# A two-layer attention and token-MLP kernel: the masks of one probability tile untied, and a new order written out by hand

## The chip, the cores and the metric

The kernel runs on one core of a Trainium2 chip. The core has five engines, each with an instruction queue of its own that it works through strictly in order: TensorE (PE, matrix products), VectorE (DVE), ScalarE (ACT), GpSimd (POOL) and SyncE (SP), which here only issues DMAs. Engines wait for one another by semaphores. The metric is the device time of one execution in microseconds; the median over several runs is compared.

## The reference, cut to what matters

```python
def _A_ref(x, wqkv, wo):                # S = 2048, D = 512
    H = 32; Dh = D // H; W = 256
    q, k, v = ...                       # x @ wqkv, 32 heads of 16
    scores = jnp.einsum("bhqd,bhkd->bhqk", q, k) * (Dh ** -0.5)
    mask = (idx[:, None] - idx[None, :] >= 0) & (idx[:, None] - idx[None, :] < W)
    p = _softmax(jnp.where(mask, scores, -1e9))
    return (p @ v, heads joined) @ wo

def _B_ref(x, w1, b1, w2, b2):          # F = 1792, mixes tokens, not features
    h = _layernorm(x)
    u = _gelu(jnp.einsum("bsd,sf->bdf", h, w1) + b1)
    return transpose(jnp.einsum("bdf,fs->bds", u, w2) + b2)

for layer in range(2):                  # the same weights in both
    x = x + _A_ref(_layernorm(x), wqkv, wo)
    x = x + _B_ref(_layernorm(x), w1, b1, w2, b2)
```

All arrays are bfloat16. Attention is causal with a window of 256 tokens, so of the 2048 x 2048 scores only a band is computed.

## The kernel before

The 2048 tokens are 16 tiles of 128; x stays in SBUF in place. Each layer's work comes in these kinds:

- **Normalise.** `ln_blocks`: statistics (L478) and their aggregate (L480) on VectorE, `rstd` (L491) on GpSimd, then `normalise` (L498) on VectorE, which writes `xh_sb`.
- **Project.** `qkv(m)` handles token block m of 512 tokens. Transposes of `xh_sb` are DMAs on SyncE (L549), or for the first block of a layer products with an identity on TensorE (L556). Then q, k and v by dense products (L520 and L522; v at L626). A key tile must be spread into a block-diagonal form with zeros between (`kbd`): for the first block straight from PSUM (L586, L588); for later blocks a copy to `stg` (L597, L599), and from there `f_kz`, eight small DMAs on SyncE (L606), or `f_kz2`, two instructions on GpSimd or VectorE (L611).
- **Attend.** `attention` works on chunks of 4 or 8 sub-blocks of 64 queries. A group of scores (L689) fills two pairs of PSUM banks; two exponentials (L704, ScalarE) write one probability tile `pt`; one or two masks (L722, GpSimd) multiply the parts of the tile at the edge of the band by 0 or 1; the products of probabilities and values (L738) follow. The value tiles carry columns of ones, so that the same product gives the sum for the softmax. `od` (L758, VectorE) transposes the result, a reciprocal (L762) and a product (L764, GpSimd or VectorE) scale it, and a last transpose (L769) makes `oT`. There are 304 exponentials, 268 masks and 64 such products in the program.
- **Mix.** `wo_block` adds the attention's output (L780). The token MLP is split: parts of its first product (`u_part`, L520) run as filler under the attention, the rest (`u_last`, L859) after it, then Gelu (L874); its second product (`y_block`, L886) of layer 0 runs under the attention of layer 1, that of layer 1 ends the program. Weights w1 and w2 are loaded by SyncE (L794, L806) into buffers that are used again and again.

The order of all this isn't that of the source. `Graph.op` records each operation with its reads and writes, from which it takes its dependences, and with a `cost`; `replay` then goes through the operations in the order that the packed string `ORDER` holds, which also picks the engine where an operation has alternatives (`alts`). So both the queue of every engine and the buffer that each tile gets are fixed by that string. The string was found off line; the costs and issue times (`cost`, `issue`) in the source are what that search used, and do nothing on the chip.

Waits follow from the recorded keys. `emit` puts a wait before an operation for each engine whose result it needs, its own engine included (TensorE with itself excepted). A mask reads and writes the two keys of its probability tile, so a second mask of that tile is recorded as depending on the first:

```python
op("gpsimd:mask", f_mask, reads=keys + LD, writes=keys, cost=100 + 2.03 * 2 * reps * nc_ * 64)
```

although the two touch different columns. Where a tile has a first mask and a second, the second waits on GpSimd's own semaphore. `f_pv`, the product of probabilities and values, waits for the last writer of the tile.

Of the kernel before, what the change touches and what calls it, by code (L numbers as in the profile page):

```python
# [11 lines left out]
P = 128  # L12
# [1 line left out]

ORDER = (
    'c-',
    'qZYKZxVX9Uj@U@8*RGOh5q@^FRj^P@zH(^gsaxR45MxRH#tlLIf9n;KBhFDqJ|Q0TCQ<;X;K2E>x&+;lhOr6)s%3*usSi7cLywfD03@*y4&UuE',
    '<Yo@2>aua_^EyNPc*w(fs}W`Mz&f8B&B$|2pvfKe!$W6E{Yk$hGkI-y_%c0@w5q#=<ZR(=fjEe2;p)q>HqBw{hQWiRQca$40XOzx~d4Tn8^a*H',
    '-7qv)NMDRm`ytHkl05L#nDm%?h01LEJH#{Yg<2X{#`dBFh>{77L-Z+Dgmp^@5&I4KEBm+hw}x+LmJKif!N9hOsvlOHqiS-',
    '0S!EA5h%yPqM79c5cyar<*Fu2ERM5*Xw3;z32N~5CjXu&^FtR#>JY-vNE5{W{$&^ah?|wE1wG4RBw%es*k4IP4Bw*c7;~UB$0!3xm=d>a_)K5E',  # L20
    'wqmBPpnB{sfF{-',
    'R1H<3lp4u{vGmBUncQr~j1L;UUfO2cR!dPrIZ~R7R&&)^HlnD|W*Rz7qG&K^^`rbIZ#LzuJDW9vI1a<09WbApoYSuxz8ApafRK<7O(Vpp5@;HG',
    '>mQWNHSM@N926o{TU8f)Uz&z#X+zE}!q}g+EHe#4$#oZs)oR_}D~i!rt>|8nDd+N($g(NR`gFSAD+*H>%d!mPbxsH=Ib;N5Ox}Ur-',
    '5p2t<|aF=w%grqo6R%GX+ehL-EO&CZkL<1n{MK?vsteg+wQhsBTZW^7YSr+u}DzzZgrfKzpu+OpH3%}MOjWJvn=x_#dJ3I2Hx1V^Dr#(-',
    '`R4W=Yv6aaDCnHr>rTPjlSFpjb>uRNjHhQQDnp&a+~b;NkY24E@?2!(q-',
    'MT9LF^X5vG1P7{(7`E5zFETEcZrLDaX?>HOQ7tiIJWt`S96(jk*&l3u%R_n=IvixoHO7?DABx6ueZ*Ymun)F~BIsGh64=vH%G%2moOe0N7=UAJ',
    'UxS(sp%$&4-M3$-',
    'juS(Xb~Hb$cqCXAq8bh~XPRISz0HSYUD2mf`!h2RcAUsYv%mGxJB6~Ln>1|~?y8e{Kq0!Q)N+gqX0Erk<coWgW^1&1h#s!k4IYf2aymn*u==xu',
    '-x!y_RW&+~kmAJA$)FN<P~kc24k`PvX7Uiz5M5GTHm5YX3PZpCz@Af$2*(>^R0`S=~}cA+yKjUkMV*2b2QQIa&9VQ5;WADF&r+NNnB#9%9KTCw',
    'MvrfOT`l5<TFnnF3yN`}2HYcL26?E6uYP{UKGEQGLaUm&$IAg>Xa&{!-',  # L30
    'Ms4T?@%OET%7@7m{s+bw&4Z=bN)1PC{yRs@gRwTez{eHj4dJ66T5o4aF{O*pwQ`0JE>GiHZ*uXdcrUxEi90a`xjeWnIgT7202V<>))HsfH6jaF',
    '}wyh|x4#h(NTMeSn98Iw-Rnrt3JQfH!Hs_ouilQG8+GzsmhHfGas)6R3u1%pN!(o3s()Fde=p-',
    'xEH0Oh&7}$<|jR*c@f*6th3f^O(3C7rOnd3Oe{Q*Qu0p>Z*;pRqR2$AV#qx1E8G~yU9`@h6^b~P>+WoJU$lSy+rH_f2P&7X}ct7Jg8ZETKFhK5',
    '534oU3#I%7RH=tBup*Nty(;+Qp^d8-vO)@fth#+9pH90XqAx7&@js;M+=+qPx-x&^TJTuTVbT;wncsUkkUzrQ!Xv-IQfXnVI6@D8$JIhJLZ<_8',
    '}X#rJ;!H-T&X%>{S;squb18rmKVgP1@8fMQ*%o9HfF7-#c>;OHT=T<-',
    'Upw);(?E_QouGa8LH>+Slx%^ImGs4Z*v`8SK@BAhqM((}~!38?RU4yd`Y?G^oXo-',
    '@6q3MFJZrXSE`@*d@Cq^hIcA>RcDISd&ajQXRD#R}mLcexWKmPO1w&$3n;1bz_0ec=1;RuuWsd>*x@h=)3FgrFpZ1l+QO1A#i&AeL<E$WWAfnQ',
    'Msk_7l9xg>d%j&aoZ9Fyq6aOoy8I6XF<v(isjrijs;rZgzgJ2}KbeMh*hJ(eW4_`~7}6B;+q^vRbVG_EYeGHlNLtWR}dPs2Gig0LZM>GK@6Miy',
    'mCD0Q^iQT@N?Hu-)O@gG;v6YH=u;8@fU?u;Zj5cqz-Oh@xoI@qj=L&*KnL;CV+(poZwUpSZr)@a_&<&%^F&z1eKm?#6JOo0Zp{qs4SKt1f7Lxm',
    'p?pNN-{Q+4_|Jsy6`Wra$yjmM{t;(r$ZEM^)P`+NM<I+_qiUb{$Y94#@PTv#I(Plm$eF7w7}V*OFw**f?oYB|X5X4d-',  # L40
    'iAX$cS>A;EQlKJdXBBZN^zaT65<#Mo%MNK}eB9Cn9E;w4=_@ZDyo>3d}*z-CeX@8I^VWCZYn#qf+Z4fw1_YGRs}YDApLc}s3)J)-',
    ')4paQQgnU?qEw%n8f$B2Lq2(hA8QRyvIWkr_DVV>XRyVV2g(Q<!WOvl|(4)qqmBZP+GXwaKZr)Y^{3JP%3DQEz(Su{=|S4?LeCLANyES*^pZvY',
    'oSG#cp|hWxg4OKmh7S{R0)#WJFxrwnO`Ae&dZtW^P21{<OO#H6Rkk57@neq=lRxa2hd;e{XjB?(s}4?l$J=fCIUtM{8XZ_dqn{b|=1%{S-',
    'PoBFHMzj|)fUU-FHe1280J$+w&I^6Tv)z#HQ2h6XXhR%^)Nmo_pDa2D+&SAaWr*=vMdVYQKq|5Kqyvy13f9d1XTY6ettK6xb+Aj~NIxC-',
    'R=a1UuNbPC3de$yiJ?tZ)&(;1k<Fmni9$v4lUa$Z7+FGq%t6zk7IdajyDE~Q%8oKOyE+M*TJtk0+9wU62cIm{32UbWI?08jHN&0;DzC2g|BddS',
    '51hq$cJbYYc_8Dc*-H(N-',
    'ov>J|J;V15v{%5b`Y^s!pO0qX7hDICsUD{`KF`E2L%}D2)i1$zQl)xb`jXhsk=8C_dJ$pm31zh_biuld^&chcldO7$jw-wtusMbL*!d9hX>FAR',
    'e5TREtNtokm%KfnR!8+u#9aSG0-nhAT*!-|r<^<tqWTj+E@ssp>tDNYqei4>Qola?<4fq7qp#Tc%-',
    'l<ntih`${UpkL%yj7_1W%X1OAV2pU4E7c=}BB9=`w^1nUP+&|FmVT_7j!$-(C86w|vR{|6f!x>C%<Y(B=Qr{s~dEH1q'
)  # L50

def begin_order(n):
# [49 lines left out]
class Graph:  # L102
# [9 lines left out]
        self.last_w = {}  # L112
        self.readers = {}

    def op(self, eng, fn, reads=(), writes=(), cost=100.0, prio=None, dma=False, after=(), holds=(), cfg=None, cls=None,
           flex=False, lock=False, issue=470.0, phase=None, alts=(), parts=1):
        o = Op()
        o.parts = parts
        eng, _, o.kind = eng.partition(":")
        o.idx, o.eng, o.fn, o.cost, o.dma = len(self.ops), eng, fn, cost, dma  # L120
        o.prio = o.idx if prio is None else prio
        o.users, o.extra = [], []
        o.cfg, o.cls, o.flex, o.lock, o.issue, o.phase = cfg, cls, flex, lock or eng == "gpsimd", issue, phase
        o.alts = [(eng, fn, cost, o.lock)] + [(a[0], a[1], a[2], len(a) > 3 and a[3] or a[0] == "gpsimd") for a in alts]
        o.cols32 = False
        deps = {}
        tiles = {}
        for key in list(reads) + list(writes) + list(holds):
            t = key[0] if isinstance(key, tuple) else key
            if isinstance(t, Tile):  # L130
                tiles[id(t)] = t
        for r in reads:
            w = self.last_w.get(r)
            if w is not None:
                deps[w.idx] = w
        for k in writes:
            w = self.last_w.get(k)
            if w is not None:
                deps[w.idx] = w
            for rd in self.readers.get(k, ()):  # L140
                deps[rd.idx] = rd
        for a in after:
            deps[a.idx] = a
        for k in writes:
            self.last_w[k] = o
            self.readers[k] = []
        for r in reads:
            self.readers.setdefault(r, []).append(o)
        deps.pop(o.idx, None)
        o.deps = list(deps.values())  # L150
        for d in o.deps:
            d.users.append(o)
        o.tiles = list(tiles.values())
        for t in o.tiles:
            t.left += 1
        self.ops.append(o)
        return o
# [155 lines left out]
def bass_interleave_layers__sliding_block__mixer_token_mlp__prompt_kernel(  # L313
# [11 lines left out]
    S, D = A_x.shape[1], A_x.shape[2]  # L325
    F = B_w1.shape[1]
# [13 lines left out]
    es = ExitStack()  # L340
    with es:
# [143 lines left out]
        def ln_blocks(ts, twice):  # L485

            t0, t1 = ts[0], ts[-1] + 1
            for t in ts:
# [1 line left out]
            keys = [f"rs{t}" for t in ts]  # L490
            op("gpsimd:rstd", lambda e: e.tensor_tensor(rstd[:, t0:t1, 0], agg[:, t0:t1, 1],  # L491
                                                        mhalf[:, 0:1].to_broadcast([P, t1 - t0]), op=ALU.pow),
               reads=[f"ag{t}" for t in ts] + ["mhalf"], writes=keys, cost=530, prio=-1e5)
            for t in ts:
                normalise(t)

# [45 lines left out]
        def qkv(m, before, split, layer):  # L542
# [3 lines left out]
            def transpose(i, wide):  # L546
                t = 4 * m + i
                if wide is None:
                    op("sync:tr", lambda e: e.dma_start_transpose(xhT[:, tx.slot, :, i * P:(i + 1) * P], xh_sb[:, t, :]),  # L549
                       reads=[f"xh{t}"], writes=[(tx, i)], dma=True, cost=900, issue=1240.0, prio=-1e5)  # L550
                    return
                ft = filler(True)

# [13 lines left out]
            def proj(o, which, a, b, wide):  # L567
# [41 lines left out]
                def f_kz2(e):  # L609
# [2 lines left out]
                                               0.0, op0=ALU.mult, op1=ALU.add)  # L612
                    return last
                op("sync:kz", f_kz, reads=[ts, "zk"] + [("par", h) for h in range(2)],
                   writes=[(tk, "k", o, h, k) for h in range(2) for k in KEYS(a, b)], cost=700, issue=4900.0, dma=True, parts=8,
                   prio=-2e5, alts=[("gpsimd", f_kz2, 1340), ("vector", f_kz2, 2 * dve_cost(n, 0.25, ptrs=1), True)])

            def vproj(sp):
# [44 lines left out]
        def attention(qs, nq, tqs, tks):  # L663
# [6 lines left out]
            for o2 in range(0, 4, 2) if nq == 4 else range(4):  # L670
# [8 lines left out]
                for su in order:  # L679
# [26 lines left out]
                            ACTF.Exp, scale=SMSCALE), reads=[ts, "acttab"], writes=[(tp, i)], cost=act_cost(2 * cols))  # L706
                    keys = [(tp, 0), (tp, 1)]
                    n = len(su)
                    masks = list(plan[su[0][0]][1])
                    while masks:  # L710
                        c0, nc_, w0 = masks.pop(0)
                        reps, cs, ws = n, half, 0
# [4 lines left out]
                        def f_mask(e, tp=tp, w=nc_ * 64, c0=c0 * 64, w0=w0 * 64, reps=reps, cs=cs, ws=ws):  # L717
# [2 lines left out]
                            part, col = [list(a) for a in m.ap]  # L720
                            m = bass.AP(m.tensor, m.offset, [part, [0, 2], [ws, reps], col])
                            return e.tensor_tensor(v, v, m, op=ALU.mult)  # L722
                        op("gpsimd:mask", f_mask, reads=keys + LD, writes=keys, cost=100 + 2.03 * 2 * reps * nc_ * 64)
                    for k, o, base in su:
                        parts[o].append((k, base, tp))

                    for o in os:
                        done[o] += sum(x[1] == o for x in su)
# [1 line left out]
                            continue  # L730

                        def f_pv(e, o=o, ps=parts[o], t=tod, i=(o - o2) * 256, st=not pvs or nq == 4):
                            pieces = sorted(((n, q0, c0, base, tp, *blk(j)) for k, base, tp in ps
                                             for j, q0, n, c0 in plan[k][0]), key=lambda x: x[0])
                            for n, q0, c0, base, tp, tk, jj in pieces:
                                for r in range(4):
# [7 lines left out]
                            return last  # L744
                        rd = list(ONES)
                        cost = -42
                        for k, base, tp in parts[o]:
                            rd += [(tp, 0), (tp, 1)]
                            for j, _, n, _ in plan[k][0]:
                                tk, jj = blk(j)  # L750
                                rd.append((tk, "v", jj))
                                cost += max(67, n * 64 / 2.4 + 3)
# [210 lines left out]
```

## Time and profile before

| | |
|---|---|
| median of 4 runs | 460.69 us (459.87 to 462.03) |
| the profiled execution | 460.79 us, its span 459.0 us, TensorE clock granted 0.996 |
| PE busy | 421.7 us (92%), 6328 products |
| ACT busy | 327.0 us (71%), of it exponentials (L704) 282.4 |
| DVE busy | 297.8 us (65%) |
| POOL busy | 234.1 us (51%), of it masks (L722) 178.8 |
| chain that ended last | PE 55%, ACT 19%, POOL 14%, DVE 6%, issue 3%, DMA 2%, SP queue 1% |

The span runs from the first to the last instruction; some 2 us of the execution lie around it. Matmuls overlap one another, so PE's busy time is no measure of how near it is to its best. The stages can be told by the engines: the start lasts until the first exponential at 12.7 us; the attention of layer 0 runs from there to 169 us, the rest of its MLP to some 215 us; the attention of layer 1 from 216 to 376 us; and the rest to 459 us is its MLP, almost all PE. The chain that ended last is followed back from the last instruction through whatever released each step; its shares say who held the end up, stage by stage, and are no busy times.

### The profile page before, as it was taken

To read this page: it belongs to the slowest core of one execution; us is meant where nothing else is said; L and a number is where in the kernel's file an instruction comes from. 1 tells how busy PE (TensorE), PEld (TensorE's weight loads), DVE (VectorE), ACT (ScalarE), POOL (GpSimd) and SP (SyncE) were. 2 spreads that over 40 slices of the span, in tenths; PEclk is the share of its full clock that TensorE was granted. 3 is DMA by queue.
4 is the path that set the end of the run, shared out by engine and by line. 5 is a ranking of instruction groups with operands and counts; after the bars stand their busy time and mean duration, and the time that the engine had idled before them with its cause. 6 is when DMAs were issued, how large, how long until landed. Compare 5 with 4: busy or idle time off the path is not lost.

```text
span 459.0 us, 14621 instructions
## 1 busy us (share of the span) xinstructions
PE 421.7 (92%) x6328; PEld 199.9 (44%) x6392; DVE 297.8 (65%) x540; ACT 327.0 (71%) x379; POOL 234.1 (51%) x345
## 2 busy tenths in 40 slices
PE   6997879899797999999999998999999999999997
PEld 5553434333343444445545443544333344444443
DVE  6798768767686559645657684779776377530234
ACT  4998979999999870533988999999999980250000
POOL 5377868757888561001448766686876760000000
PEclk9999989999999999999999999999999999999999
DMA  8242453100044237560142124224313237672435
GB/s 254 68 50 61 81 101 88 22 6 1 4 115 107 75 91 200 142 186 1 47 73 82 23 52 62 57 48 103 80 43 93 78 92 203 171 219 58 125 100 164
DMA packets 98591, 41.59 MB, mean 91 GB/s; under 512 B 37088, under 2 KB 98528, under 8 KB 98528
## 3 DMA queue, kind: packets, MB, share of 16 engines
q1 hardware_dynamic: 98528, 40.67, 34.7%
q8 instruction: 50, 0.82, 0.8%
q14 instruction: 13, 0.11, 0.1%
HBM read 33.56 MB, written 2.10 MB: 78 GB/s over the span
## 4 chain that ended last, share of the span: by engine, by line
PE 55%; ACT 19%; POOL 14%; DVE 6%; issue 3%; DMA 2%; SPq 1%; POOLq 0%
PE PS L520 34%; ACT pt L704 18%; POOL pt L722 12%; PE PS L859 8%; PE PS L689 5%; PE PS L738 5%; PE PS L626 2%; DVE xh_sb L498 2%; DMA xhT<-xh_sb 2%; DVE rl L758 1%; POOL ul L764 1%; PE PS L522 1%; SPq L549 1%; POOL rstd L491 1%; ACT kbd L588 1%
## 5 line engine op out<-in xcount | busy, mean ns | idle before, releaser
L704 ACT ACTIVATE pt<-PS 128x1024 bf16<-128x1024 f32 (+1 forms) x304 | 282.4, 1037 | 21.1 <-PE PS L689 20.2
L722 POOL TENSOR_TENSOR pt<-pt,ldm 128x256 int32<-128x256 int32 (+1 forms) x268 | 178.8, 682 | 87.1 <-ACT pt L704 80.8
L520 PE MATMUL PS<-xh_sb,w1b 128*128 128x512 bf16 x259 | 65.2, 380 | 5.0 <-issue 3.0
L689 PE MATMUL PS<-qT,kbd 32*128 32x256 bf16 (+4 forms) x1488 | 61.0, 253 | 6.8 <-ACT pt L704 1.6
L520 PE MATMUL PS<-uT,w2b 128*128 128x512 bf16 x259 | 63.7, 380 | 1.4 <-issue 1.1
L520 PE MATMUL PS<-xhT,wqkv 128*128 128x512 bf16 (+1 forms) x248 | 60.5, 369 | 4.7 <-issue 2.7
L886 DVE SCALAR_TENSOR_TENSOR x_sb<-PS,b2col,x_sb 128x512 bf16<-128x512 f32 x32 | 23.3, 746 | 58.4 <-PE PS L520 58.2
L758 DVE STREAM_TRANSPOSE rl<-PS 128x1024 f32<-128x1024 f32 x32 | 39.9, 1246 | 25.3 <-PE PS L738 25.3
L491 POOL TENSOR_TENSOR rstd<-agg,mhalf 128x2 f32<-128x2 f32 (+1 forms) x33 | 22.9, 701 | 59.3 <-DVE agg L480 53.0
L738 PE MATMUL PS<-pt,vb 64*32 64x320 bf16 (+4 forms) x2976 | 45.6, 253 | 8.0 <-POOL pt L722 7.2
L689 PEld LDWEIGHTS PS<-qT,kbd 32*128 32x128 bf16 x1488 | 21.9, 92 | 62.4 <-ACT pt L704 47.5
L874 ACT ACTIVATE uT<-rl,b1col 128x512 bf16<-128x512 f32 x28 | 18.2, 712 | 41.9 <-DVE rl L870 41.7
L478 DVE BATCH_NORM_STATS2 stats<-x_sb 128x6 f32<-128x512 bf16 x64 | 42.5, 678 | 0.3
L498 DVE TENSOR_SCALAR xh_sb<-x_sb,agg,rstd 128x512 bf16<-128x512 bf16 x64 | 33.1, 536 | 11.7 <-POOL rstd L491 11.7
L738 PEld LDWEIGHTS PS<-pt,vb 64*32 64x32 bf16 x2976 | 28.6, 89 | 27.7 <-POOL pt L722 16.6
L520 PE MATMUL PS<-uT,pt 128*128 128x512 bf16 x165 | 39.4, 379 | 0.2
L520 PEld LDWEIGHTS PS<-uT,w2b 128*128 128x128 bf16 x272 | 24.8, 98 | 31.0 <-issue 3.8
L520 PEld LDWEIGHTS PS<-xh_sb,w1b 128*128 128x128 bf16 x280 | 23.4, 98 | 34.0 <-issue 7.0
L859 PE MATMUL PS<-xh_sb,w1b 128*128 128x512 bf16 x165 | 37.1, 379 | 0.3
L520 PEld LDWEIGHTS PS<-xhT,wqkv 128*128 128x128 bf16 x266 | 22.9, 101 | 29.1 <-issue 7.4
L626 PE MATMUL PS<-wqkv,xhT 128*64 128x256 bf16 x512 | 34.7, 278 | 0.9 <-DVE rl L758 0.5
L520 PE MATMUL PS<-wo_sb,oT 128*128 128x512 bf16 x116 | 29.4, 380 | 1.6 <-ACT pt L704 0.9
(64 smaller groups left out, 343.2 us busy)
## 6 DMA issues: line engine op xcount, KB each, us to landing
w1b<-in_B_w_dram SPq DMA_DIRECT2D x112, 128.0 KB, 2.7
w2b<-in_B_w_dram SPq DMA_DIRECT2D x70, 128.0 KB, 2.6
pt<-in_B_w_dram SPq DMA_DIRECT2D x42, 128.0 KB, 2.9
out_dram<-x_sb SPq DMA_DIRECT2D x16, 128.0 KB, 2.0
kbd<-stg SPq DMA_DIRECT2D x112, 16.0 KB, 1.9
x_sb<-in_A_x_dram SPq DMA_DIRECT2D x3, 512.0 KB, 7.4
wqkv<-in_A_wqkv_dram SPq DMA_DIRECT2D x4, 256.0 KB, 4.3
wqkv<-in_A_wqkv_dram SPq DMA_DIRECT2D x1, 512.0 KB, 6.8
```

The costliest lines, as they stand in the source:

```text
L478: op("vector:stat", lambda e: e.bn_stats(st[:, 0:6], x_sb[:, t, :]), reads=[f"x{t}"], writes=[("st", i)], cost=dve_cost(512), after=late_s ...
L491: op("gpsimd:rstd", lambda e: e.tensor_tensor(rstd[:, t0:t1, 0], agg[:, t0:t1, 1], mhalf[:, 0:1].to_broadcast([P, t1 - t0]), op=ALU.pow), ...
L498: op("vector:xh", lambda e: e.tensor_scalar(xh_sb[:, t, :], x_sb[:, t, :], agg[:, t, 0:1], rstd[:, t, :], op0=ALU.subtract, op1=ALU.mult), ...
L520: return e.matmul(o, lhsT=w, rhs=x, start=start, stop=stop, skip_group_check=True)
L626: last = e.matmul(bank(ft)[64 * j:64 * j + 64, sc * 256:(sc + 1) * 256], lhsT=xhT[:, tx.slot, c, tok:tok + 64], rhs=wqkv[:, c, 1024:1536]. ...
L689: last = e.matmul(bank(tt[r // 2], r % 2)[:, base + c0 * 64:base + (c0 + n) * 64], lhsT=kbd[32 * r:32 * r + 32, tk.slot, o, jj].rearrange( ...
L704: op("scalar:exp", lambda e, ts=ts, tp=tp, i=i, cols=cols: e.activation(probs(tp)[:, i, 0:cols, :], pair(ts)[:, :, 0:cols].rearrange("p r ...
L722: return e.tensor_tensor(v, v, m, op=ALU.mult)
L738: last = e.matmul(bank(t, h)[32 * r:32 * r + 32, i + q0 * 64:i + (q0 + n) * 64], lhsT=vb[64 * h:64 * h + 64, tk.slot, jj, 4 * o + r, :], r ...
L758: op("vector:od", lambda e, t=tod, tr=tr: e.transpose(rl[:, tr.slot:tr.slot + 2].rearrange("p a b -> p (a b)"), pair(t)), reads=[(tod, i) ...
L859: last = e.matmul(bank(tu, tt), lhsT=v()[:, sc - b0, k0 + tt * P:k0 + (tt + 1) * P], rhs=xh_sb[:, sc, :], start=(sc == b0), stop=(sc == NT ...
L886: op("vector:resy", lambda e: e.scalar_tensor_tensor(x_sb[:, t, :], bank(ft), b2col[:, t:t + 1], x_sb[:, t, :], op0=ALU.add, op1=ALU.add), ...
```

## The change

It has three parts.

The masks of one tile get keys of their own. A mask no longer writes the tile's keys, but one named by its first column; the product reads the tile's two keys and all the masks' keys. So a second mask depends on the exponentials alone.

The costs that the search used are changed: the default from 100 to 200, `rstd` from 530 to 640, a mask from 100 + 2.03 per column to 143 + 2.115, a DMA transpose's issue from 1240 to 1350 and the issue of eight key DMAs from 4900 to 5600. For 256 columns a mask's cost goes from 620 to 684.

The string `ORDER` is a new one, and with it every queue. The operations are the same 2457. Some are on another engine: key expansions from `stg` are 15 on SyncE, 2 on GpSimd and 7 on VectorE (before: 14, 6 and 4); the scaling products of L764 are 16 on GpSimd and 16 on VectorE (before: 20 and 12); of the three fills of ones two are on GpSimd and one on ScalarE (before: one on VectorE, two on ScalarE); of the copies of key tiles 4 are on ScalarE (before 7), of those of value tiles 5 (before 3). The waits of GpSimd on its own semaphore fall from 104 to 5. TensorE's queue has 915 groups in both, changing from one kind of product to another 346 times before and 345 after.

```diff
 ORDER = (
     'c-',
-    'qZYKZxVX9Uj@U@8*RGOh5q@^FRj^P@zH(^gsaxR45MxRH#tlLIf9n;KBhFDqJ|Q0TCQ<;X;K2E>x&+;lhOr6)s%3*usSi7cLywfD03@*y4&UuE',
...
+    'qBQF^KER6&>00{+|aEn85s?4+@Bn3Vl#Og$fr6I3R)oD)c~w3l|C~Ac6`NE>x&cp@0Y~RJd@030t_>!i5V5T)1%IVha}zxNzaZ#THv^;lhQBSL',
...
-    def op(self, eng, fn, reads=(), writes=(), cost=100.0, prio=None, dma=False, after=(), holds=(), cfg=None, cls=None,
+    def op(self, eng, fn, reads=(), writes=(), cost=200.0, prio=None, dma=False, after=(), holds=(), cfg=None, cls=None,
...
-               reads=[f"ag{t}" for t in ts] + ["mhalf"], writes=keys, cost=530, prio=-1e5)
+               reads=[f"ag{t}" for t in ts] + ["mhalf"], writes=keys, cost=640, prio=-1e5)
...
-                       reads=[f"xh{t}"], writes=[(tx, i)], dma=True, cost=900, issue=1240.0, prio=-1e5)
+                       reads=[f"xh{t}"], writes=[(tx, i)], dma=True, cost=500, issue=1350.0, prio=-1e5)
...
-                   writes=[(tk, "k", o, h, k) for h in range(2) for k in KEYS(a, b)], cost=700, issue=4900.0, dma=True, parts=8,
+                   writes=[(tk, "k", o, h, k) for h in range(2) for k in KEYS(a, b)], cost=700, issue=5600.0, dma=True, parts=8,
...
-                    masks = list(plan[su[0][0]][1])
+                    masks, mk = list(plan[su[0][0]][1]), []
...
-                        op("gpsimd:mask", f_mask, reads=keys + LD, writes=keys, cost=100 + 2.03 * 2 * reps * nc_ * 64)
+                        mk.append((tp, "m", c0))
+                        op("gpsimd:mask", f_mask, reads=keys + LD, writes=mk[-1:], cost=143 + 2.115 * 2 * reps * nc_ * 64)
                     for k, o, base in su:
-                        parts[o].append((k, base, tp))
+                        parts[o].append((k, base, tp, mk))
...
-                        for k, base, tp in parts[o]:
-                            rd += [(tp, 0), (tp, 1)]
+                        for k, base, tp, mk in parts[o]:
+                            rd += [(tp, 0), (tp, 1), *mk]
```

In the new queues, at the places that the prediction comes to: at the start VectorE takes the statistics before the mask tables, and GpSimd both first `rstd` before its second zeroing of `kbd`; TensorE does four projections instead of three before the first scores. In the third token block SyncE issues two key sets and then the four transposes, where before the last transpose stood behind a key set.

## The prediction

> **What bounds the kernel now.** I read the page's busy shares first, then the engines by stretch, then the table of who waits for whom, and last the timelines of the places that these point to. Busy shares by stretch (columns: stretch, its length, then busy time of PE, weight load, VectorE, ScalarE and GpSimd with their counts, granted clock, DMA share, GB/s):
>
> ```profile
> 12.00:40.00 28.00, 23.87 (x550) 14.60 (x544) 22.73 (x52) 26.43 (x39) 16.81 (x24) 1.00 0.28 48
> 40.00:80.00 40.00, 34.63 (x750) 17.00 (x754) 31.59 (x58) 35.86 (x40) 30.41 (x44) 0.96 0.41 90
> ...
> 172.00:212.00 40.00, 39.84 (x193) 18.16 (x194) 28.54 (x56) 10.99 (x16) 2.76 (x4) 1.00 0.54 152
> ...
> 260.00:280.00 20.00, 19.36 (x347) 8.16 (x348) 16.51 (x29) 18.75 (x21) 13.53 (x22) 1.00 0.38 60
> ```
>
> In layer 1 (fourth row) and in the MLP (third) PE is full: work moved about inside them gains nothing. In the attention of layer 0 (first two rows) PE has holes and ScalarE, with two exponentials of 0.904 us from start to start per group of scores, is at 90 to 94%. So a better order can win only in about the first 150 us. What stands in the holes, by the waits (total us, times, longest):
>
> ```profile
> ACT pt L704 <- PE PS L689: 20.2, 33, 1.9
> ...
> DVE xh_sb L498 <- POOL rstd L491: 11.7, 11, 4.0
> ...
> PE PS L738 <- POOL pt L722: 7.2, 17, 1.1
> ...
> PE PS L522 <- DMA xhT<-xh_sb: 1.9, 1, 1.9
> ```
>
> The exponentials starve for scores 33 times; the probability products (L738) wait 17 times for GpSimd's masks; once PE waits for a transpose. At four places the timelines show what lies behind this (start, length, engine, line, then the idle time before it):
>
> ```profile
> 6.11 1.86 DVE L498 TENSOR_SCALAR xh_sb<-x_sb,agg,rstd 128x512 bf16<-128x512 bf16 x1 [0.46 <-POOL rstd L491]
> ```
> ```profile
> 6.03 1.80 POOL L460 MEMSET kbd<- 128x2048 f32 x1
> ```
> ```profile
> 38.27 0.60 SPq L424 DMA_DIRECT2D wo_sb<-in_A_wo_dram  x1
> 44.81 0.82 SPq L794 DMA_DIRECT2D w1b<-in_B_w_dram  x2
> ...
> 51.49 5.51 SPq L606 DMA_DIRECT2D kbd<-stg  x8
> 57.05 6.19 SPq L549 DMA_TRANSPOSE xhT<-xh_sb  x3
> ```
> ```profile
> 61.08 1.05 PE L522 MATMUL PS<-xhT,wqkv 128*64 128x512 bf16 x8 [1.85 <-DMA xhT<-xh_sb]
> ```
>
> **Step A, the start.** Before, VectorE does the ones (0.91) and the first mask table (0.87) ahead of the first statistics (L478 at 3.35), and GpSimd's second zeroing begins as the second normalise does: that takes 1.86 us and ends at 7.97, the memset at 7.83. The first dense product then starts at 9.16, the first scores at 11.83. After, VectorE's queue has the statistics first, and both rstd and both normalises stand before the second zeroing. Tile 0 lands at 0.79 + 2.1 = 2.9; statistics 0.70 and aggregate 0.19: 3.8; GpSimd's first zeroing ends about then; two rstd of 0.61: 5.1; the second normalise, 0.4: 5.5. PE's warm-up runs until 5.8; two transposes, 0.6; copies out on ScalarE (0.59) and VectorE (0.42) at once: the first product at about 7.0, 2.2 earlier. A fourth group of projections (0.6 to 0.8) now stands before the first scores, part of it under copies that they wait for: 0.5 off. **-1.7**.
> [...] The row: the normalise under the memset took 1.86 where the quickest takes 0.31. [...] After, the copy of a transposed tile (0.42; no row shows one beside a memset) and the mask tables meet the zeroing and one set of ones on GpSimd. By the row alone the copy is free: -2.2. [...] I take the value nearer the row, since the copy reads PSUM as the statistics read SBUF, and those ran at 0.70 under the first zeroing.
> [...]
>
> **Step B, SyncE's queue.** Before, a set of eight key DMAs (5.51) is queued ahead of the last transposes of the third token block; PE waits 1.85 and the exponentials 0.77 + 1.86 + 0.45 + 0.30 = 3.4 between 58 and 67 us. After, the order is two key sets, three weight loads, then all four transposes, with weight loads between, then the disputed key set. The second key set goes into a hole: the first ended at 38.2 and the queue slept until 44.81 but for one load of 0.60; 38.2 + 5.6 = 43.8. Then three loads (1.4), four transposes (5.0) and two loads (0.9): 52.1, and 2.6 to landing, 54.7, against a consumer that stood at 61.08 - 1.85 = 59.2, or 57.5 with A. Even if the inputs are normalised 2 us later it is in time. The disputed set: 52.1 + 0.5 + 5.6 + 1.9 to landing = 60.1; its scores come 7.1 us of PE work after 57.5. The stall goes; what is late next is ScalarE, which has its exponentials to make up. **-2.0** (0 to -3.4).
> The other transposes and key sets: 14 key sets on SyncE become 15, GpSimd's fall from 6 to 2. The tightest is the last of layer 1: behind weight loads which wait for a buffer that a dense group frees about 10 us of PE work ahead of the scores; 5 loads of 0.5, 5.6 and 1.9 make 10.0. Its sets measured 5.1 to 6.7, so up to **+1** here; I take +0.5.
>
> **Step C, masks.** 100 of the 268 masks wait on GpSimd's own semaphore; after, none. From the trace's start times: a 256-column mask is followed after 0.68 if the next waits for nothing, 0.80 to 0.81 if it waits for the mask itself (62 cases); for 128 columns 0.41 and 0.53. So 100 x 0.12 = 12 us of GpSimd's 234; with 4 key sets of 1.33 and 4 products of 1.01 gone to others and two fills of 0.95 come, its load falls by some 20. On the path lies only the last mask before a product: 17 waits x 0.12 = **-2.0**; at most all 7.2, at least nothing, if the backlog was not the cause.
>
> **Step D, PE.** Both orders hold the same 915 groups. A change from dense products to scores or to probability products costs 0.31 (738 against 431 ns for the same pair of matmuls): dense to scores falls from 93 to 85, dense to probabilities rises from 24 to 28, probabilities to scores (0.27) from 32 to 36, and the rest about cancels: under 0.2 us. [...]
>
> Sum: -1.7 + 0.5 - 2.0 + 0.5 - 2.0 = -4.7. From the profiled execution, 460.79 (span 459.0 and 1.8 around it), that is 456.1; the median of the runs is 0.1 lower: **456.0**.
>
> **Rivals.** (1) Slower: the probability products become the new wait. In each order I added the PE work between the last scores of a product and the product itself, and against it two exponentials, their masks and what GpSimd has queued between. PE's work falls short in 11 of 64 products before (12.4 us) and in 17 after (17.5); in layer 1, where PE has no hole to hide it, 0.6 becomes 6.2. The measured waits there add to 2.25. If the shortfall counts in full, +5.7; the start and the transposes still give -3.7, and the rest +1.0, so 460.7 + 3.0 = 463.7. It decides from where PE's waits for masks in layer 1 pass some 5 us. Against it: the count knows nothing of ScalarE's own queue, which spreads the groups, and GpSimd has 20 us less to do. (2) Hidden: ScalarE is the bound of layer 0, and time won early is lost at the next shortage; A gives -0.1, B and C half of theirs, and the costs of A and B stay: -0.1 - 1.0 - 1.0 + 1.0 = -1.1, so 459.6. For it: 16 of the 20 us of starved exponentials have no single cause. (3) The plan fits: all of A, B and C, -2.2 - 3.4 - 7.2, at 447.9. For it: the new mask costs (684 and 414 ns by the formula) are what the trace shows undisturbed, where the old said 620 and 360; against it, no plan empties every hole.
>
> **Numbers.** Forecast 0.50 (its own range 452.5 to 459), rival (1) 0.25, (2) 0.17, (3) 0.08. A measurement of this kernel tells about 0.3% from no change: 459.3 to 462.1. Faster: 0.50 + 0.08 + 0.05 of (2) = 0.63; same: 0.10 of (2) and 0.02 of (1), 0.12; slower 0.25. The range of 8 in 10 leaves out (3) and the far half of (1): 451.5 to 463.
>
> **What would show it.** A: first scores (L689) near 10 us, the second normalise near 0.4 us. B: no wait of PE for a transpose around 57 to 61, exponentials without gaps there. C: masks of 128x256 following one another at 0.68, PE's wait for L722 under 5.2 in sum. The forecast is wrong if that wait grows, if gaps of the exponentials sum to over 20 us again, or if layer 1, from the first scores after 212 us to the end, grows by more than 2 us.

## The result, and the profile after

| | median | range | ratio to before, 95% interval |
|---|---|---|---|
| before | 460.74 us (63 runs) | 457.36 to 463.1 | |
| after | 458.49 us (44 runs) | 455.16 to 462.72 | 0.9948 [0.9935, 0.9961] |

The change made the kernel faster by 2.3 us, a half of one per cent; the forecast was 456.0 us, 4.7 us less than before. The profiled execution of after took 461.32 us (span 459.3), one of its longest: the two pages' totals can't be set against each other, and what follows reads single places, then settles them with timed kernels.

The table of waits of after (engine and line, whom it waited for: total us, times, longest), the last two rows from the same table of PE's own stream:

```profile
ACT pt L705 <- PE PS L690: 21.6, 38, 4.2
...
PE PS L521 <- DMA xhT<-xh_sb: 3.5, 2, 2.7
PE PS L740 <- POOL pt L723: 0.5, 2, 0.3
```

The probability products (L740, before L738) waited 7.2 us for masks before, 0.5 now: step C shows at once. But the exponentials starve for scores as long as before (21.6 against 20.2 us), the longest gap has grown to 4.2 us, and PE waits longer for transposes (over all its lines 4.2 us in 3 waits; before, 3.1 in 2). Busy shares by stretch of after, columns as in the prediction, and the last stretch of before under them:

```profile
12.00:40.00 28.00, 22.62 (x564) 14.96 (x568) 24.23 (x56) 26.72 (x39) 16.81 (x24) 0.99 0.36 66
40.00:80.00 40.00, 34.09 (x727) 16.76 (x728) 31.10 (x62) 35.12 (x39) 27.06 (x39) 0.96 0.39 79
80.00:120.00 40.00, 35.71 (x728) 15.21 (x715) 28.67 (x47) 37.93 (x42) 26.02 (x40) 0.96 0.12 16
```
```profile
80.00:120.00 40.00, 35.70 (x703) 15.63 (x710) 28.43 (x45) 38.23 (x42) 29.08 (x43) 1.00 0.05 9
```

In these stretches of layer 0 PE has as many holes as before, and the recorded granted clock is below 1 in each of the three (before: 1.00, 0.96, 1.00). The start shows part of why (timeline of after: start, length, engine, line, idle time before it):

```profile
4.79 3.54 DVE L499 TENSOR_SCALAR xh_sb<-x_sb,agg,rstd 128x512 bf16<-128x512 bf16 x2
...
5.50 0.95 POOL L465 MEMSET vb<- 128x1024 f32 x1
6.38 1.80 POOL L461 MEMSET kbd<- 128x2048 f32 x1
...
8.39 0.40 PE L557 MATMUL PS<-ident,xh_sb 128*128 128x128 bf16 x4 [2.34 <-DVE xh_sb L499]
9.31 3.49 PE L521 MATMUL PS<-xhT,wqkv 128*128 128x256 bf16 x16 [0.52 <-DVE xhT L564]
12.73 0.40 PE L690 MATMUL PS<-qT,kbd 32*128 32x256 bf16 x12
```

The same products before:

```profile
9.16 2.74 PE L520 MATMUL PS<-xhT,wqkv 128*128 128x256 bf16 x12 [0.52 <-DVE xhT L563]
11.83 0.61 PE L689 MATMUL PS<-qT,kbd 32*128 32x256 bf16 x12
```

After's two normalises as one group of that line (shortest, median and longest in ns):

```profile
L499 DVE TENSOR_SCALAR xh_sb<-x_sb,agg,rstd x2: 402/1703/3004, 4.8 to 5.3; 128x512 bf16<-128x512 bf16 x2
```

The first normalise took 0.40 us, the second 3.00: it began at 5.32, and ended at 8.33, with two fills of GpSimd that lie wholly within it, 0.15 us after the second. The first scores stand at 12.73, where before had them at 11.83: the first dense product comes 0.15 us later, and 16 of them take 3.49 where 12 took 2.74. At 0.22 to 0.23 us for a product, both run at about half the pace that the cured starts below show (0.12 to 0.13). Before has no clock on record until 14.65 us, so the 1.00 of its row from 12 to 40 us doesn't count that slow start. The second place, SyncE's queue and what waits for it (timelines of SP, PE and ACT in after):

```profile
34.90 11.64 SPq L607 DMA_DIRECT2D kbd<-stg  x16
46.59 2.78 SPq L796 DMA_DIRECT2D w1b<-in_B_w_dram  x3
49.41 1.23 SPq L550 DMA_TRANSPOSE xhT<-xh_sb  x1
...
51.79 5.02 SPq L550 DMA_TRANSPOSE xhT<-xh_sb  x3
...
60.34 2.32 PE L521 MATMUL PS<-xhT,wqkv 128*128 128x512 bf16 x5 [2.73 <-DMA xhT<-xh_sb]
...
63.26 1.94 ACT L705 ACTIVATE pt<-PS 128x1024 bf16<-128x1024 f32 x2 [4.18 <-PE PS L690]
```

The two key sets start 2.4 us later than the first of them did before, take 11.6 us together, and the last transpose lands after PE has stood for 2.73 us.

So the gain came in spite of A and B. The experiments take each apart. The theories behind them: M, the untied masks made the whole gain; L, a hold of VectorE by GpSimd's fills made the start late, so that both normalises, kept clear of the fills, take near the first one's 0.40 us; Q, the key sets made the transposes late; H, a hole of PE costs more than its length, since a stretch at half clock follows (after's record has three of 3.4 us, from 9.15, 60.35 and 84.25).

### The profile page after: what moved, and what is told of

It is laid out like the page before. It is cut to its first block, busy times and chain, and to the rows that moved or that the text cites. A ratio compares the mean times of both kernels' runs of the same rounds, so it can differ in the third digit from the quotient of the medians.

```text
span 459.3 us, 14679 instructions
## 1 busy us (share of the span) xinstructions
PE 420.4 (92%) x6346; PEld 201.8 (44%) x6412; DVE 302.1 (66%) x551; ACT 325.9 (71%) x377; POOL 224.5 (49%) x335
## 4 chain that ended last, share of the span: by engine, by line
PE 62%; ACT 12%; DVE 11%; SPq 6%; DMA 5%; issue 2%; POOL 2%
PE PS L521 41%; ACT pt L705 11%; PE PS L861 7%; PE PS L690 6%; PE PS L740 5%; SPq L607 3%; DVE xh_sb L499 3%; PE PS L627 3%; DMA xhT<-xh_sb 2%; DVE stats L479 2%; DVE x_sb L782 2%; DVE rl L760 2%; SPq L796 1%; POOL pt L723 1%; SPq L550 1%
## 5 line engine op out<-in xcount | busy, mean ns | idle before, releaser
L705 ACT ACTIVATE pt<-PS 128x1024 bf16<-128x1024 f32 (+1 forms) x304 | 282.6, 1038 | 22.6 <-PE PS L690 21.6
L723 POOL TENSOR_TENSOR pt<-pt,ldm 128x256 int32<-128x256 int32 (+2 forms) x268 | 176.5, 680 | 98.0 <-ACT pt L705 94.6
L521 PE MATMUL PS<-xh_sb,w1b 128*128 128x512 bf16 x259 | 67.0, 387 | 5.3 <-ACT pt L705 2.9
L521 PE MATMUL PS<-uT,w2b 128*128 128x512 bf16 x267 | 66.7, 380 | 1.5 <-issue 0.8
L521 PE MATMUL PS<-xhT,wqkv 128*128 128x512 bf16 (+1 forms) x233 | 56.1, 369 | 8.7 <-DMA xhT<-xh_sb 3.5
L740 PE MATMUL PS<-pt,vb 64*32 64x320 bf16 (+4 forms) x2976 | 44.8, 253 | 1.5 <-ACT pt L705 0.6
L861 PE MATMUL PS<-xh_sb,w1b 128*128 128x512 bf16 x164 | 37.4, 379 | 0.8 <-DMA w1b<-in_B_w_dram 0.5
L740 PEld LDWEIGHTS PS<-pt,vb 64*32 64x32 bf16 x2976 | 29.4, 90 | 19.2 <-POOL pt L723 8.2
L499 DVE TENSOR_SCALAR xh_sb<-x_sb,agg,rstd 128x512 bf16<-128x512 bf16 x64 | 30.8, 509 | 8.2 <-POOL rstd L492 8.1
L627 PEld LDWEIGHTS PS<-wqkv,xhT 128*64 128x64 bf16 x512 | 25.5, 109 | 10.3 <-issue 3.6
```

Of the source, the lines that this page charges most:

```text
L499: op("vector:xh", lambda e: e.tensor_scalar(xh_sb[:, t, :], x_sb[:, t, :], agg[:, t, 0:1], rstd[:, t, :], op0=ALU.subtract, op1=ALU.mult), ...
L521: return e.matmul(o, lhsT=w, rhs=x, start=start, stop=stop, skip_group_check=True)
L627: last = e.matmul(bank(ft)[64 * j:64 * j + 64, sc * 256:(sc + 1) * 256], lhsT=xhT[:, tx.slot, c, tok:tok + 64], rhs=wqkv[:, c, 1024:1536]. ...
L705: op("scalar:exp", lambda e, ts=ts, tp=tp, i=i, cols=cols: e.activation(probs(tp)[:, i, 0:cols, :], pair(ts)[:, :, 0:cols].rearrange("p r ...
L740: last = e.matmul(bank(t, h)[32 * r:32 * r + 32, i + q0 * 64:i + (q0 + n) * 64], lhsT=vb[64 * h:64 * h + 64, tk.slot, jj, 4 * o + r, :], r ...
L861: last = e.matmul(bank(tu, tt), lhsT=v()[:, sc - b0, k0 + tt * P:k0 + (tt + 1) * P], rhs=xh_sb[:, sc, :], start=(sc == b0), stop=(sc == NT ...
```

## The experiments

**Untied masks alone, in the old order.** The kernel before, with its old `ORDER` and the mask edit of the change and nothing else:

```diff
-op("gpsimd:mask", f_mask, reads=keys + LD, writes=keys, ...)
+mk.append((tp, "m", c0))
+op("gpsimd:mask", f_mask, reads=keys + LD, writes=mk[-1:], ...)
...
+rd += [(tp, 0), (tp, 1), *mk]
```

> The old order with the masks of a tile untied: the dependence alone. If the masks' waits on each other are the gain (theory M): 1.5 to 3 us faster than before (ratio 0.9935 to 0.997), TensorE's own waits for L722 down from 7.2 us to under 4, and 256-column masks in a row 0.68 us apart. If the new order is the gain (theory O): within 1 us of before (0.998 to 1.001), the time that masks give back being taken by the next wait, mostly ScalarE's exponentials.

458.29 us (12 runs), ratio 0.9948 [0.9927, 0.9969]: the very ratio of the whole change. PE's waits for the masks in this kernel:

```profile
PE PS L739 <- POOL pt L722: 4.4, 13, 0.9
```

7.2 us in 17 waits became 4.4 in 13; those 2.8 us cover the gain of 2.2. In layer 1 the waits fell from 2.5 to 1.0 us, and layer 1 is 1.7 us shorter (table below).

**The new order with the masks tied again.** The kernel after, each second mask waiting for the first of its tile:

```diff
+if o.kind == "mask":
+    o.extra += [x for x in o.tiles[0].ops if x.kind == "mask" and x is not o][-1:]
```

> The new order with each mask made to wait again for the one before it of the same tile. Theory M: the gain is gone or nearly (ratio to before 0.998 to 1.003), and TensorE's waits for the masks are back at 5 us or more. Theory O: still 2 us or so faster than before (0.994 to 0.997).

459.47 us (12 runs), ratio 0.998 [0.9953, 1.0007]. The order alone may be worth 1 us or nothing: the interval takes in both. With the first run: untied masks are worth 2.2 us in the old order; in the new the medians differ by 1.0, not clear of the noise, and PE waits for masks only 2.2 us even when they are tied.

**The fills behind the normalises.** The kernel after, with GpSimd's fill of ones (operation 35) and its second zeroing (33) made to wait for the first two normalises:

```diff
+first = [o for o in self.ops if o.kind == "xh"][:2]
+for o in self.ops:
+    if o.idx in (35, 33):
+        o.extra += first
```

> The new order, but the set of ones and the second zeroing on GpSimd wait until the first two normalises are done. [...]

455.95 us (6 runs), ratio 0.9892 [0.9854, 0.9929]. The timeline of its start:

```profile
4.72 0.95 DVE L503 TENSOR_SCALAR xh_sb<-x_sb,agg,rstd 128x512 bf16<-128x512 bf16 x2
6.68 0.42 DVE L568 COPY xhT<-PS 128x512 bf16<-128x512 bf16 x1 [1.01 <-PE PS L561]
...
6.62 1.80 POOL L465 MEMSET kbd<- 128x2048 f32 x1
...
7.16 2.07 PE L525 MATMUL PS<-xhT,wqkv 128*128 128x256 bf16 x16 [0.52 <-DVE xhT L568]
9.35 0.40 PE L694 MATMUL PS<-qT,kbd 32*128 32x256 bf16 x12
```

The two normalises take 0.95 us together instead of 3.54. The copy out of PSUM, which begins 0.06 us after the zeroing and runs wholly under it, still takes 0.42: it isn't held. So the fills held the second normalise (SBUF to SBUF, 3.00 us beside them) and not the copy. The first scores come at 9.35, 3.4 us earlier; the median gains 2.5.

**The same in the old order.** There the second zeroing alone held a normalise (1.86 us). The kernel of the first experiment, with the edit above for operation 33 only:

```diff
+    if o.idx == 33:
+        o.extra += first
```

> The old order with the masks untied, as in e1, and the second zeroing on GpSimd behind the first two normalises. [...]

455.56 us (6 runs), ratio 0.9898 [0.9862, 0.9933]; the second normalise takes 0.41 us instead of 1.86, and the first scores stand at 9.29. The old order gains 2.7 us by the same cure (2.3 by the ratios, each to its own session's runs of before) and stands beside the new one. Here, too, part of the gain is pace: 12 dense products take 1.48 us where they took 2.64 in the first experiment.

**Products in the start's hole.** The kernel after, the late normalise left as it is, but PE kept at work with 18 products of the identity, into columns that nothing reads, between the two groups of transposes:

```diff
+for _ in range(18 if t == 0 and not layer else 0):
+    last = e.matmul(bank(ft)[:, 256:384], lhsT=ident[:], rhs=ident[:], start=True, stop=True)
```

> The changed kernel with 18 more products with the identity in the hole at the start, where TensorE waits 2.3 us for the second normalise; their result is read by nobody. If the slow products behind the hole come from the clock (theory H): no stretch at half clock from 9 to 12.5 us, 16 dense products there take near 2.1 us instead of 3.5, the first scores come about 1 us earlier than 12.7, and 0.5 to 1.3 us come off the changed kernel (ratio 0.992 to 0.9940). Rival, they are slow since their inputs come late: no change (0.9945 to 0.996).

457.19 us (9 runs), ratio 0.9932 [0.9908, 0.9957]. PE's timeline:

```profile
6.01 1.84 PE L560 MATMUL PS<-ident 128*128 128x128 bf16 x18
8.40 0.40 PE L557 MATMUL PS<-ident,xh_sb 128*128 128x128 bf16 x4 [0.55 <-DVE xh_sb L499]
9.32 1.92 PE L521 MATMUL PS<-xhT,wqkv 128*128 128x256 bf16 x16 [0.52 <-DVE xhT L566]
11.35 0.40 PE L692 MATMUL PS<-qT,kbd 32*128 32x256 bf16 x12
```

The dense products start where they did (9.32 against 9.31), and 16 of them take 1.92 us where after took 3.49. The stretch from 8 to 13 us in after and, under it, in this kernel (the next to last three columns are the granted clock, DMA share and GB/s):

```profile
8.00:13.00 5.00, 4.09 (x32) 2.69 (x32) 2.65 (x8) 1.37 (x4) 0.19 (x1) 0.66 1.06 358
```
```profile
8.00:13.00 5.00, 3.96 (x44) 3.15 (x45) 3.49 (x12) 3.40 (x8) 0.20 (x1) 1.00 1.09 357
```

A mean of 0.66 over 5 us is 3.4 us at half clock. The hole of 2.34 us had it follow; filled, it doesn't come. That is 1.6 us of dense products and 1.4 of the first scores. What it is worth in the whole is less sure: the medians differ by 1.3 us, the ratios by 0.7, and their intervals overlap.

**The second key set behind the transposes.** The kernel after, with the second of the two sets moved on SyncE to just behind the four transposes and the third set (a helper in `begin_order`'s result moves one operation behind another):

```diff
-g.replay(begin_order(len(g.ops)))
+g.replay(behind(begin_order(len(g.ops)), 204, 197))
```

> The new order with one key set of eight DMAs (needed only some 27 us of TensorE work later) moved behind the four transposes of the third token block and behind the key set needed first. If SyncE's queue makes the 2.7 us wait (theory Q): that wait and the 4.2 us hole of the exponentials go, and 1.5 to 2.7 us come off the changed kernel (ratio to before 0.989 to 0.992). Rival: the hole only moves, since the normalises behind the transposes are as late, or a key set is now late; then 0.994 to 0.996, with a wait of the same length for the transposes or for key tiles.

462.13 us (12 runs), ratio 1.0036 [1.0013, 1.0059]: slower. The wait at 60 us went (ScalarE's gap there fell from 4.18 to 0.46 us), but everything behind it on SyncE moved, and 25 us later this stood there (timelines of PE and ACT):

```profile
85.00 2.74 PE L529 MATMUL PS<-xh_sb,w1b 128*128 128x512 bf16 x6 [3.91 <-DMA w1b<-in_B_w_dram]
...
88.24 14.95 ACT L713 ACTIVATE pt<-PS 128x1024 bf16<-128x1024 f32 x16 [5.06 <-PE PS L698]
```

Two weight loads, issued at 82.65 behind a key set and two transposes, came late for products that had been early enough before. PE's granted clock was 0.62 on average from 80 to 89 us, which is 6.8 us at a half: as long as this hole and 3 us of products behind it, and those six took 2.74 us where the next six took 1.47.

**Three moves on SyncE.** The kernel just shown, with those two loads placed ahead of the next key set and that set behind the four transposes after it:

```diff
+for k, at in ((502, 532), (534, 502), (457, 691)):
+    order = behind(order, k, at)
```

> The new order with SyncE's queue re-sorted in one place: the key set that is needed late goes behind the one needed early, two weight loads go up behind their neighbours, and the next key set goes behind the four transposes of the fourth block. If e5 was slow only because two weight loads then stood behind what had been put off (theory Q): no wait of TensorE over 1 us for a DMA between 50 and 100 us, 2 to 4 us off the changed kernel (ratio to before 0.986 to 0.991). Rival, SyncE has too much to do in this stretch in any order: a wait of 1.5 us or more for some DMA stays, ratio 0.993 or more.

456.57 us (6 runs), ratio 0.9912 [0.9886, 0.9939]. PE waits for no DMA between 50 and 100 us, and the time is 1.9 us under after's (1.7 by the ratios): about that is what SyncE's order cost.

**Both cures in the new order**, the moves and the fills together, run twice:

> e7 and e3 together. If the two holes are independent: both gains add, 4 to 6 us off the changed kernel, ratio to before 0.981 to 0.986, and the granted clock is 0.996 or better in most runs. Rival: with the start 2.4 us earlier SyncE is late again at the third block: then no better than e3 (0.987 to 0.991).

> The new order with three key sets and two fills moved, a second time beside the old order cured in the same way: 452.8 us (451.5 to 454), ratio 0.983 (0.980 to 0.986); under one half-clock stretch per run.

452.84 us, ratio 0.983 [0.9798, 0.9861], and 452.69 us, ratio 0.9837 [0.9806, 0.9868] (6 runs each): faster than both kernels, by 5.7 us than after. First scores at 8.75 us.

**Both cures in the old order.** The kernel with the old order, the untied masks and the later zeroing, and its key set of 49.5 us moved behind the transpose that PE waited for:

```diff
-g.replay(begin_order(len(g.ops)))
+g.replay(behind(begin_order(len(g.ops)), 197, 433))
```

> The old order with the masks untied, the second zeroing behind the first two normalises, and now SyncE's key set of 49.5 us behind the transpose that PE waited 1.76 us for at 59.3. Theory H (holes, not the order, cost the time): the wait of PE for a transpose near 59 goes, first scores stay at 9.3, fewer half-clock stretches; 454.0 us (452.5 to 455.5), ratio 0.986; the new order with the same cures, 452.8, is then worth 1 us at most. Rival O (the new order is worth something of its own): no more than 0.5 us below 455.6, so over 2 us above the cured new order. Rival N (the key set becomes the new wait): PE or ScalarE waits over 1 us for scores between 56 and 66 us, 455.5 to 457.

453.12 us (6 runs), ratio 0.9852 [0.9823, 0.9881], in the same session as the second run above. Timelines of SP and PE, with the same product in the kernel with the later zeroing alone under them:

```profile
44.72 4.90 SPq L561 DMA_TRANSPOSE xhT<-xh_sb  x3
49.66 5.45 SPq L618 DMA_DIRECT2D kbd<-stg  x8
...
56.10 1.03 PE L534 MATMUL PS<-xhT,wqkv 128*64 128x512 bf16 x8
```
```profile
59.26 1.05 PE L526 MATMUL PS<-xhT,wqkv 128*64 128x512 bf16 x8 [1.76 <-DMA xhT<-xh_sb]
```

The product that stood at 59.26 behind a wait of 1.76 us now starts at 56.10 with none, and PE waits for no key set between 40 and 110 us. With these holes gone, the old order comes within 0.4 us of the new, and the intervals overlap. The rival that gave the new order over 2 us of its own falls; a value below what these runs can tell isn't excluded.

**Where the new order gives back what it wins.** First scores of layer 1, and the rest to the end, from one profile each (us):

| | first scores of layer 1 | from there to the end |
|---|---|---|
| before | 215.8 | 243.2 |
| old order, untied | 214.7 | 241.5 |
| old order, both cures | 209.3 | 241.7 |
| after | 214.7 | 244.6 |
| new order, tied | 211.0 | 244.5 |
| new order, both cures | 207.3 and 208.1 | 244.8 and 244.6 |

Layer 1 repeats from profile to profile (244.0 to 245.3 in all eight of the new order, 241.5 to 241.8 in the three of the old with untied masks); the other column holds the half-clock stretches, three in after's profile. In the old order the untied masks take 1.7 us off layer 1. The new order is about 3 us longer there whether the masks are tied or not. From the first exponential of layer 1 on, PE waits 1.0 us for DMAs in the old order untied; in after it is 4.3 us, of it 2.0 for key sets and 1.5 for transposes. In the two profiles with both cures the key waits are 0.5 and 1.0, yet layer 1 takes as long; what stands in their place, beside a hole of 1.1 us without a named cause in the first of them, wasn't settled. Since the totals are level, the cured new order is ahead of the old when layer 1 begins, by 1.2 and 2.0 us, and loses it there.

## Why the prediction was right in sign and short in size

**The opening reading was too narrow.** It closed layer 1 ("work moved about inside them gains nothing"), but the untied masks took 1.7 us off layer 1. It counted one wait of PE for a transpose; before's table has a second, of 1.2 us, in layer 1. And it has no term for the slow products of before's start, which the clock row doesn't show.

**Step A, forecast -1.7, came out near +0.9** by the profiles (first scores 11.83 to 12.73). The step that failed is "the second normalise, 0.4: 5.5": the step overlooked that GpSimd, free of the second zeroing until both rstd were done, would start a fill of ones at 5.50, 0.18 us after the second normalise, and the zeroing after that, at 6.38. The normalise, begun before the first fill, ended behind both, at 8.33: 3.00 us, where the first took 0.40. The prediction asked what the zeroing does to the copy, which the third experiment showed free (0.42), as it had taken it, and not what it does to the normalise, for which its own row (1.86 us under a memset) spoke. So the first product, forecast 2.2 us earlier, came 0.15 later, and the fourth group of projections, forecast at 0.5, cost 0.75 at half pace. That pace is a term that the sum had nowhere: before had it at its start as well, so it isn't what made after later, but it is 1.6 us that a start without the hole would win. With the fills moved the first product stood at 7.16, against 7.0 in the forecast, and the first scores at 9.35, better than the 10 forecast, since 16 products took 2.07 us. The mechanism of the step was right, and was blocked.

**Step A's +0.5 for the instructions that move to VectorE** is a term of the sum that no run shows. In its place, the two profiles show their length: the scaling products there have a median of 0.69 us and a longest of 0.79 (before 0.69 and 1.02), the instructions of the key expansions 0.34 and 1.20 (before 0.55 and 0.82). No wait in the profile of after points to a cost of theirs.

**Step B, forecast -2.0, was a loss.** The step's sum had the second key set ending at 43.8; it ended at 46.5, since the first started at 34.9 and not 32.5 and the pair took 11.6 us; "three loads (1.4)" took 2.8. Landing was put at 54.7; the last transpose was issued by 56.8, and PE's wait ended at 60.3. The wait grew from 1.85 to 2.73 us and the exponentials' gap there to 4.18. (The sum itself slips by 1.0: 43.8 + 1.4 + 5.0 + 0.9 is 51.1, not 52.1.) Moving the sets won 1.9 us against after; as PE's wait there was 0.9 longer in after than before, some 1.0 of that, an estimate, is a gain on before, half of the 2.0 forecast. The first attempt to cure it, slower by 0.36%, and the second, with the same transfers and no wait, show that it was the order of SyncE's queue that counted, up to 25 us on, and not the amount in it.

**The last key set, forecast +0.5, was too small.** Two waits of 1.0 us for key sets stand in layer 1 of after, where before shows none that long; with the transposes it is part of the 3 us that the new order takes more there.

**Step C, forecast -2.0, held:** -2.2 by the first experiment (1.4 to 3.4 by its interval). 17 waits x 0.12 us was the right size of the median; the waits themselves fell by 2.8 in the old order, and to 0.5 in the new, where the load of GpSimd also fell (busy 234.1 to 224.5 us).

**Step D, forecast under 0.2, was not tested:** no run was made for it, and PE's part of the longer layer 1 that isn't a wait for a DMA is open. So are PE's holes put down to "issue" in the trace, time for which no cause is shown (before: 1.07 us ahead of the scores at 38.76, 0.16 ahead of the dense products at 39.23).

**The rivals.** The first, mask waits growing in layer 1, failed: they were 2.5 us there before and at most 0.5 in the whole of after. The count of PE work between scores and products, on which it stood, doesn't see what spreads the groups, as the prediction warned. Layer 1 did grow, by 1.4 us against before, but not by waits for masks. The second, won time hidden by ScalarE, fell with the cures: 5.7 us came off. No run shows its -0.1 for A; A itself came out near +0.9. The third named 447.9 for all of A, B and C; with A and B mended it was 452.7.

By its own test ("gaps of the exponentials sum to over 20 us again") the forecast was wrong about layer 0: the gaps sum to 21.6. That it came out inside its range is luck as far as A and B go: C alone carried the gain, and A and B, which were to bring 3.7 of the 4.7 us, brought none together with the rest of the order.

## What to carry to other kernels

When an edit moves an engine's work earlier, list what the other engines then have free to start at once, and look in the traces for what it did to that work when they last ran side by side (here a memset had made a normalise 1.86 us long); the fill that had been in the way came back through the gap that the edit opened. Cost an issue queue as a whole and to its end: a set of DMAs moved out of one wait goes in front of another (a wait of 2.73 us at 60 went, one of 3.91 us at 85 came). And before giving a new schedule the credit, put the one-line part of the change into the old one: here it gave all of the gain, and two moves in the old order were worth more than the whole change.

## What the runs showed of the hardware

**A hole of PE can cost more than its length.** In nine of the twelve profiles the record of PE's clock has a half for 3.4 us (once 6.8) while there is work: in after from 9.15, 60.35 and 84.25 us, in before from 62.4. Two profiles show a slow start that this record lacks: before, whose clock is first recorded, as full, at 14.65, and the kernel with three moves on SyncE (16 dense products in 3.59 us, with 1.00 on its row from 8 to 14 us). At the start the hole decides: the six profiles in which PE stood 1.7 to 2.3 us for the second normalise had a slow start (four show it by their products, 0.22 to 0.23 us each; the tied new order and the slower kernel of the SyncE experiment by a granted clock of 0.88 and 0.89 over the first 12 us). Of the six without that hole, five show their first dense products, at full pace or nearly: 16 in 1.92 to 2.07 us, or 12 in 1.48.

Later on a hole doesn't always bring a stretch. Near 60 us holes of 1.85, 1.91 and 2.73 us (before, old order untied, after) had one begin in them or within 1.4 us; behind holes of 1.76 (old order with the later zeroing) and 2.47 us (new order with the fills moved) none came:

```profile
57.26 1.47 PE L525 MATMUL PS<-xhT,wqkv 128*128 128x512 bf16 x6 [2.47 <-DMA xhT<-xh_sb]
```

And the one at 84.25 in after stands behind three short holes, 0.59, 0.61 and 0.83 us. What else decides, these runs don't show. At the start, after's hole of 2.34 us had one behind it, and filling that hole took the stretch away (granted clock from 8 to 13 us 0.66, then 1.00).

From the mean granted clock of each run (one such stretch lowers it by 0.0037; a slow start as in before isn't in it), after had on average 1.6 stretches, the slower kernel of the SyncE experiment 3.7, both cures in the new order 0.2 and 0.8, and in the old order 0.4. The kernel with the filled hole had 1.9: it lost the stretch at the start in its profile, but not in number. Among the runs of after, those with none had a mean of 457.07 us (8 runs), those with three 460.87 (7): about 1.3 us each, though the holes that bring them count in it too.

**A normalise was held to the end of two fills, and a copy was not held.** The normalise, from SBUF to SBUF, met two fills and ended behind both, 3.00 us instead of 0.40, though it had begun 0.18 us before the first. A copy from PSUM to SBUF under the same zeroing kept its 0.42; that its source makes the difference wasn't tested by itself.

**Two masks of 256 columns without a tie follow one another at 0.68 to 0.69 us** (after), 1.42 for a pair of which the last takes 0.73. Tied (before), the second started 0.80 us behind the first, and the pair took 1.53.
